# Rounding of layer 2's weights moved to chunks 1 and 8 to 10, with clamp and sign on GpSimd, and seven block products in chunk 7

## The chip, the core and the metric

The kernel runs on one core of a Trainium2 chip. The metric is device time in microseconds (us) of one execution; lower is better. TensorE does the matrix products, ScalarE, VectorE and GpSimd prepare their operands, and SyncE's queue (SP) issues nearly all transfers.

## What is computed

The reference has three stages on `x` of shape 2 x 3008 x 256 in float32:

```python
X = np.fft.rfft(x, axis=1)                      # spectral layer
Yr = Xr @ w_r - Xi @ w_i + b_r
Yi = Xr @ w_i + Xi @ w_r + b_i
Y  = sign(Y) * max(|Y| - 0.01, 0)               # on Yr and Yi
y  = np.fft.irfft(Y, n=3008, axis=1)            # 6016 tokens of 256
h = y @ w_in;  g = h / (1 + exp(-h));     y2 = g @ w_out     # layer 1, 256 -> 2048 -> 256
h = y2 @ w_in2; g = max(0.01 * h, h);     out = g @ w_out2   # layer 2, same sizes
```

## The kernel before, in words

**Arithmetic.** Every product of float32 matrices is made of three TensorE products of parts: each operand is split into a high part `hi` (rounded to the type TensorE multiplies) and the rest `lo`, and `lo*hi + hi*lo + hi*hi` is accumulated in PSUM. The high part is made by ScalarE (a cast), the low part by VectorE or GpSimd (a subtraction). The weights are first rounded to fewer bits, which takes some integer work; the change is about when and where this is done for layer 2.

**Stages.** After the forward DFT, the spectral layer and the start of the inverse DFT, the two layers run over 12 chunks of up to 512 tokens (chunk 11 has 384), each over 8 pairs of 128-wide slices of the 2048 hidden columns. The loop at L1033 counts these pairs through both layers, i = 0 to 191; chunk c of layer 1 is pairs 8c to 8c + 7. It is a software pipeline written out by hand: in the turn of pair i (`pr`) its first product is formed, pair i - 1 (`one`) is activated and split, and the second product of pair i - 2 (`two`) is accumulated. The order of calls is the order on every engine's queue.

**First product.** In an ordinary pair `first` (L723) does 2 x 6 matmuls of 512 columns. In a "quick" pair `seven` (L683) does seven block products instead of eight, in Strassen's manner: 7 x 3 matmuls of 256 columns, with sums of the weights (`sums_in`) and differences of the input (`sum_x2`, L521) prepared ahead, and with `keep` (three ScalarE copies) and `join` (two VectorE additions) to put the blocks together. Which chunks are quick is set by `FIRST_QUICK` and `LAST_QUICK` (L33, L34): 3 to 6 in layer 1, 2 to 10 in layer 2. Quick turns are written out in `quick_turn` (L974) and end with `continue`.

**Second product.** From chunk 2 of layer 1 on all chunks but the last of a layer use seven block products here (21 matmuls of 256 columns, L801). Its operands are T1 (`t1`, L769: VectorE in layer 1's chunks after the last quick one, else GpSimd), T2 and T3 (L776), T4 (L782), high parts by ScalarE (L794) and low parts (L757) by VectorE, for the group "a" by GpSimd. Chunks 0 and 1 are "plain": ScalarE casts (L762), VectorE subtracts, 12 matmuls of 512 columns. In chunk 1 GpSimd also forms sums of layer 1's weights (`sums_w1`, L588 and L601) and ScalarE and VectorE split them (L594, L595) and prepare `sums_in` (`sum_first`, L630).

**Inverse DFT.** In layer 1, `invert_next` (L571) ends the inverse for the chunk after the next in the first turns of a chunk: up to 8 small matmuls (L481), a VectorE copy (L494) and a store in a turn.

**Rounding of layer 2's weights.** They are cut into 32 pieces. A piece is loaded (`load`, L140, 256 KB, SP), ScalarE makes `c` and `m` from its two halves (L147, L149), VectorE clamps `m` (L152), shifts and masks it (L154) and puts in the sign bit of the raw data (L159), GpSimd adds `c` and `m` (L165), and SP stores the result to DRAM (L167, 128 KB). `single` (L213) does one piece in each turn from pair 55 to pair 88 (`R0`, `ROUND`, L960), the add at the start of the next turn, the rest at its end through `background` (L964). The rounded weights are loaded from DRAM by `load_m` (L947) at the pairs in `LOAD` (L958), and layer 2's sums are made from them at pairs that `PLAN` (L930) lists, counted from pair 88 on.

The memory of the weight sums (`hold0`, `hold1` of the two homes) is free once layer 1's last quick chunk has read them; `load_m` uses it for the rounded weights.

## Time and profile before

| | |
|---|---|
| median of 3 runs | 1119.71 us (1119.35 to 1120.61) |
| the profiled execution, its own time | 1119.13 us |
| its span, first to last instruction | 1117.4 us |
| TensorE busy | 1112.1 us, 100% of the span |
| VectorE busy | 950.0 us, 85% |
| ScalarE busy | 878.8 us, 79% |
| GpSimd busy | 655.0 us, 59% |

In the profile PE is TensorE's matmuls, PEld its weight loads, DVE is VectorE, ACT ScalarE, POOL GpSimd, SP SyncE. Times are in us, durations of one instruction in ns. L801 is line 801 of the kernel; where a helper issues all instructions of a kind they share its line. A releaser behind `<-` is what ended an engine's idle time. In the rows of busy times by stretch the last three columns are the granted clock of TensorE, the busy share of the DMA engines and GB/s. A matmul's end in the profile is modelled, so a TensorE that is busy for all of a stretch may still have small gaps in it.

### The profile page before, as it was taken

The page shows a single profiled execution, that of the slowest core. Times are in us where ns is not written, and L with a number is a line of the kernel's source. Part 1 is how long each engine was busy: PE and PEld are TensorE (multiplying, and loading weights), DVE is VectorE, ACT ScalarE, POOL GpSimd, SP SyncE. Part 2 cuts the span into 40 slices and gives each one's busy share as a digit, 9 for nine tenths or more (in the row PEclk, how much of TensorE's full clock was granted, in tenths as well). Part 3 has the DMA queues.
Part 4 walks back from the last instruction along what each step waited for, and adds up shares of the span by engine and source line. Part 5 has one row for each costly group of instructions (what it writes and reads, how often), then busy time and mean ns, then how long its engine had stood idle before and what let it go on. Part 6 is the DMA issues. An engine that isn't in the chain of part 4 may idle for free.

```text
span 1117.4 us, 23034 instructions
## 1 busy us (share of the span) xinstructions
PE 1112.1 (100%) x8220; PEld 1057.2 (95%) x8220; DVE 950.0 (85%) x1654; ACT 878.8 (79%) x1928; POOL 655.0 (59%) x684
## 2 busy tenths in 40 slices
PE   9999999999999999999999999999999999999998
PEld 9899888889999999999999998999999999999998
DVE  4898966578888899889999888989999999999973
ACT  4788877566788888677777777789888988988874
POOL 0567845645577565334444435756876786688652
PEclk9999999999999999999999999999999999999999
DMA  9445544123112102423344310100100101010000
GB/s 233 147 143 171 168 148 130 58 75 98 41 45 84 57 19 79 130 93 115 116 123 146 119 34 1 39 30 30 37 22 21 39 20 39 21 39 21 34 15 20
DMA packets 52547, 83.70 MB, mean 75 GB/s; under 512 B 5712, under 2 KB 27824, under 8 KB 52432
## 3 DMA queue, kind: packets, MB, share of 16 engines
q1 hardware_dynamic: 52144, 82.04, 23.9%
q8 instruction: 65, 1.06, 0.4%
q14 instruction: 50, 0.41, 0.1%
q10 hardware_dynamic: 288, 0.18, 0.1%
HBM read 52.71 MB, written 29.49 MB: 74 GB/s over the span
## 4 chain that ended last, share of the span: by engine, by line
PE 99%; DVE 0%; issue 0%; ACT 0%; POOL 0%; POOLq 0%; DVEq 0%
PE acc L801 41%; PE ph L730 20%; PE px L699 13%; PE py L699 10%; PE pz L353 6%; PE py L382 3%; PE pa L305 3%; PE px L481 2%; PE pb L405 1%; PE warm L293 0%; DVE winlo L625 0%; POOL yl L397 0%; DVE zl L366 0%; ACT ph L721 0%; DVE x L490 0%
## 5 line engine op out<-in xcount | busy, mean ns | idle before, releaser
L757 POOL TENSOR_TENSOR x<-u,x 128x512 fp32r<-128x512 f32 (+1 forms) x176 | 228.0, 1296 | 174.6 <-ACT x L794 166.7
L801 PE MATMUL acc<-x,whi 128*128 128x256 f32 (+1 forms) x1696 | 315.9, 280 | 0.0
L801 PEld LDWEIGHTS acc<-x,whi 128*128 128x128 f32 x1696 | 259.9, 189 | 0.0
L801 PE MATMUL acc<-x,wlo 128*128 128x256 f32 (+1 forms) x848 | 239.3, 282 | 0.0
L757 DVE TENSOR_TENSOR x<-v,x 128x768 fp32r<-128x768 f32 (+1 forms) x176 | 213.0, 1210 | 25.5 <-ACT x L794 24.7
L794 ACT CAST x<-v 128x768 fp32r<-128x768 f32 (+1 forms) x176 | 143.0, 813 | 48.0 <-DVE v L782 47.0
L730 PE MATMUL ph<-x,winhi 128*128 128x512 f32 (+1 forms) x704 | 179.9, 376 | 0.0
L801 PEld LDWEIGHTS acc<-x,wlo 128*128 128x128 f32 x848 | 160.4, 189 | 1.3
L730 PEld LDWEIGHTS ph<-x,winhi 128*128 128x128 f32 x704 | 130.7, 188 | 21.3
L769 POOL TENSOR_TENSOR u<-u 128x256 f32<-128x256 f32 x128 | 105.2, 822 | 59.4 <-ACT u L721 36.9
L801 PE MATMUL acc<-h,whi 128*128 128x256 f32 (+1 forms) x672 | 125.0, 279 | 0.0
L794 ACT CAST x<-u 128x512 fp32r<-128x512 f32 (+1 forms) x176 | 110.3, 627 | 3.2 <-PE acc L801 1.7
L776 DVE TENSOR_TENSOR v<-px,u 128x512 f32<-128x512 f32 x104 | 71.7, 689 | 40.8 <-ACT h L794 26.2
L730 PE MATMUL ph<-x,winlo 128*128 128x512 f32 (+1 forms) x352 | 105.4, 379 | 0.1
L801 PEld LDWEIGHTS acc<-h,whi 128*128 128x128 f32 x672 | 102.4, 189 | 2.1
L703 ACT COPY u<-px 128x256 f32<-128x256 f32 x208 | 80.0, 385 | 24.7 <-PE px L699 23.7
L165 POOL TENSOR_TENSOR wc<-wc,wm 128x256 uint32<-128x256 uint32 x64 | 49.3, 771 | 81.9 <-ACT x L794 40.2
L801 PE MATMUL acc<-h,wlo 128*128 128x256 f32 (+1 forms) x336 | 93.6, 279 | 0.0
L699 PE MATMUL px<-x,shi 128*128 128x256 f32 x416 | 81.3, 278 | 0.0
L699 PE MATMUL px<-x,winhi 128*128 128x256 f32 x416 | 81.3, 277 | 0.0
L699 PE MATMUL py<-x,shi 128*128 128x256 f32 x416 | 81.3, 277 | 0.0
L709 DVE TENSOR_TENSOR u<-py,u 128x512 f32<-128x512 f32 x104 | 71.7, 689 | 0.3 <-issue 0.3
(155 smaller groups left out, 2918.2 us busy)
## 6 DMA issues: line engine op xcount, KB each, us to landing
x2i<-scr SPq DMA_DIRECT2D x38, 256.0 KB
wraw<-in_moe_w_in_dram SPq DMA_DIRECT2D x32, 256.0 KB
wraw<-in_moe_w_out_dram SPq DMA_DIRECT2D x32, 256.0 KB
scr<-bo SPq DMA_DIRECT2D x48, 128.0 KB
scr<-x2o SPq DMA_DIRECT2D x22, 256.0 KB
out_dram<-x2o SPq DMA_DIRECT2D x22, 256.0 KB
dmr<-in_dm_dram SPq DMA_DIRECT2D x34, 160.0 KB
bt<-scr SPq DMA_DIRECT2D x14, 384.0 KB
```

The lines of the kernel that those rows point to most:

```text
L165: add.tensor_tensor(out=c, in0=c, in1=m, op=ALU.add)
L305: nc.tensor.matmul(pa[h][:, s * 128:(s + 1) * 128], lhsT=xt[c][:, s, h * 128:(h + 1) * 128], rhs=da_sb, start=True, stop=True, skip_group_ ...
L353: nc.tensor.matmul(turned(pz), lhsT=u[:, h, :], rhs=turned(v[:, h].rearrange("p g e -> p (g e)")), start=(n == 0), stop=(n == len(terms) - 1))
L699: nc.tensor.matmul(turned(out), lhsT=x, rhs=turned(y), start=(k in (1, 5) and i == 0), stop=(i == 2), skip_group_check=True)
L703: nc.scalar.copy(self.u[:, a:a + 256], src)
L709: nc.vector.tensor_tensor(out=u, in0=cols(self.py), in1=u, op=ALU.add)
L730: nc.tensor.matmul(turned(ph), lhsT=u[:, h, f % HALF * 128:][:, :128], rhs=turned(v[:, h, :]), start=(i == 0), stop=(i == len(terms) - 1))
L757: eng.tensor_tensor(out=lo, in0=src, in1=hi.bitcast(F32), op=ALU.subtract)
L769: (nc.vector if self.layer == 1 and self.c > LAST_QUICK[1] else nc.gpsimd).tensor_tensor(out=blk(1), in0=blk(0), in1=blk(2), op=ALU.subtract)
L776: nc.vector.tensor_tensor(out=cols(v), in0=b22, in1=cols(u), op=ALU.subtract)
L794: nc.scalar.copy(hi, src)
L801: nc.tensor.matmul(turned(dst), lhsT=u, rhs=turned(v), start=(begin and self.p == 0 and i == 0), stop=(end and self.p == NF // 2 - 1 and i ...
```

## The change

Layer 1's chunk 7 becomes quick (`LAST_QUICK`). The rounding of layer 2's weights gets a class of its own. Its 32 pieces are the same and come in the same order, but a piece now goes through its steps in different half turns: load; two activations on ScalarE; clamp and sign on GpSimd; one VectorE instruction that shifts `m` and puts the sign in; the add on GpSimd and the store. The sign is now made as a number: -2^31 where `m` is negative, written as an integer into the raw buffer. `round_turn` is called twice in a turn, at its start and after the first products; 5 pieces go through in pairs 8 to 15 (two sets of buffers in memory that is used otherwise from pair 16 on), 27 in pairs 64 to 90 (four sets, in the memory of the weight sums of the second home), five pieces in four pairs. The loads of `load_m(0)` come at pairs 76, 78, 80 and 82.

```diff
@@ -31,7 +32,7 @@
 NF = DFF // 128
 KT = 14
 FIRST_QUICK = {1: 3, 2: 2}
-LAST_QUICK = {1: 6, 2: 10}
+LAST_QUICK = {1: 7, 2: 10}
 
 
 def turned(a):
...
-        def single(early=False):
-            if early:
-                if scaled:
-                    around(nc.gpsimd)
-                return
-            if loaded:
-                list(begin())
-                list(scale())
-            elif not made:
-                load()
-                made.append(1)
-            load()
...
+    class Rounding:
+
+        def __init__(self, pieces):
+            self.pieces, self.loaded, self.begun, self.bound, self.scaled = pieces, [], [], [], []
+            self.n = 0
+
+        def house(self, raws, ms, cs):
+            self.raws, self.ms, self.cs = raws, ms, cs
+
+        def load(self):
+            if self.pieces:
+                src, dst = self.pieces.pop(0)
+                raw = self.raws[self.n % len(self.raws)]
+                nc.sync.dma_start(out=raw, in_=src)
+                self.loaded.append((raw, self.ms[self.n % len(self.ms)], self.cs[self.n % len(self.cs)], dst))
+                self.n += 1
+
+        def turn(self, new, more):
+            done = self.scaled
+            self.scaled = []
+            if self.bound:
+                raw, m, c, dst = self.bound.pop(0)
+                nc.vector.scalar_tensor_tensor(out=m, in0=m, scalar=3, in1=raw[:, :256], op0=ALU.logical_shift_left, op1=ALU.bitwise_or)
+                self.scaled.append((raw, m, c, dst))
+            for _ in range(more):
+                self.load()
+            for raw, m, c, dst in done:
+                nc.gpsimd.tensor_tensor(out=c, in0=c, in1=m, op=ALU.add)
+                nc.sync.dma_start(out=dst()[0], in_=c.bitcast(F32))
+            if self.begun:
+                raw, m, c, dst = self.begun.pop(0)
+                nc.gpsimd.tensor_scalar(out=m.bitcast(F32), in0=m.bitcast(F32), scalar1=MAG, scalar2=-MAG, op0=ALU.min, op1=ALU.max)
+                nc.gpsimd.tensor_scalar(out=raw[:, :256].bitcast(I32), in0=m.bitcast(F32), scalar1=0.0, scalar2=-2.0 ** 31, op0=ALU.is_lt, op1=ALU.mult)
+                self.bound.append((raw, m, c, dst))
+            if new and self.loaded:
+                raw, m, c, dst = self.loaded.pop(0)
+                two = raw.rearrange("p (e w) -> p e w", w=2)
+                nc.scalar.activation(out=c, in_=two[:, :, 0], func=ACTF.Copy, scale=2.0 ** -29)
+                nc.scalar.activation(out=m.bitcast(F32), in_=two[:, :, 1].bitcast(F32), func=ACTF.Copy, scale=2.0 ** -112)
+                self.begun.append((raw, m, c, dst))
 
     raws, late = [stage], {}
-    load_w, step_w, fifth_w, until_w = weight_pieces(
-        w_in1, w_out1, lambda k: [w_in[k][p] for p in parts] + [scr_w[:, :, k * DFF // 2:][:, :, :DFF // 2]], lambda k: [w_out[k][p] for p in parts], 2, NF)
+    load_w, step_w, fifth_w, until_w = weight_pieces(list_pieces(
+        w_in1, w_out1, lambda k: [w_in[k][p] for p in parts] + [scr_w[:, :, k * DFF // 2:][:, :, :DFF // 2]], lambda k: [w_out[k][p] for p in parts]), NF)
+    dst_m = lambda q, n: lambda k: [scr_m[q][:, k].rearrange("p (d c) -> p d c", d=2) if n else scr_m[q][:, k]]
+    rounding = Rounding(list_pieces(w_in2, w_out2, dst_m(0, 1), dst_m(1, 0)))
 
 
     fs, right = ExitStack(), ExitStack()
@@ -942,7 +969,7 @@
         if todo and (make := todo.pop(0)):
             make()
 
-    closing = []
+    closing, early = [], ExitStack()
 
     def load_m(k):
         m = [homes[k].tile([128, DFF], F32, tag=f"hold{n}", name=f"m_{q}") for n, q in enumerate(("in", "out"))]
@@ -955,21 +982,27 @@
             nc.sync.dma_start(out=m_in[k][:, :, j * 512:][:, :, :512], in_=src[0][:, :, j * 512:][:, :, :512])
             yield
 
-    LOAD = [(load_m(0), [77, 79, 81, 83]), (load_m(1), [90, 91, 92, 93])]
+    LOAD = [(load_m(0), [76, 78, 80, 82]), (load_m(1), [90, 91, 92, 93])]
     FIRST = [(sum_first(k), w) for k, w in enumerate(([10, 11, 12, 13, 13], [13, 14, 14, 15, 15], [16, 17, 17, 18, 18], [18, 19, 20, 21, 21]))]
-    R0 = 8 * LAST_QUICK[1] + 7
-    ROUND = range(R0, R0 + 34)
-    rounds = []
+    EARLY, LATE = 8, 8 * LAST_QUICK[1] + 8
+
+    def houses(tiles, n):
+        flat = [t[:, a:a + w].bitcast(U32) for t, w, k in tiles for a in range(0, w * k, w)]
+        rounding.house(flat[:n], flat[n::2], flat[n + 1::2])
+
+    def round_turn(i, half):
+        k = 2 * i + half
+        if EARLY * 2 <= k < EARLY * 2 + 16:
+            k -= EARLY * 2
+            rounding.turn(k in (2, 4, 7, 9, 12), 2 if k == 0 else k in (5, 7, 10))
+        elif LATE * 2 <= k < LATE * 2 + 54:
+            k -= LATE * 2
+            rounding.turn(k > 2 and (k % 2 == 1 or k % 8 == 0), 2 if k == 0 else k > 2 and (k % 2 == 1 or k % 8 == 0))
 
     def background(i):
-        if i == R0:
-            dst = lambda q, n: lambda k: [scr_m[q][:, k].rearrange("p (d c) -> p d c", d=2) if n else scr_m[q][:, k]]
-            rounds.append(weight_pieces(w_in2, w_out2, dst(0, 1), dst(1, 0), 1)[1])
         for steps, when in FIRST + LOAD:
             for _ in range(when.count(i)):
                 next(steps)
-        if i in ROUND:
-            rounds[0]()
 
     def quick_turn(pr, one, two, i):
         last = pr.p == NF // 2 - 1
@@ -1031,8 +1064,12 @@
             make_next()
 
     for i in range(len(pairs) + 2):
-        if rounds and i in ROUND:
-            rounds[0](True)
+        if i == 16:
+            early.close()
+            late["m4"] = pool("late4", 1, **near).tile([128, 2 * 1024 + 12], F32R, name="h1")
+        if i == LATE:
+            houses([(homes[1].tile([128, DFF], F32, tag="hold0", name="round"), 512, 4), (homes[1].tile([128, DFF], F32, tag="hold1", name="round"), 256, 8)], 4)
+        round_turn(i, 0)
         pr = pairs[i] if i < len(pairs) else None
         one, two = blocks(i - 1), blocks(i - 2)
 
@@ -1056,7 +1093,8 @@
                 both = pool("big2", 1, **near)
                 for q in parts:
                     late[q] = both.tile([128, NF // 2, 7, 128], F32R, name=f"w{q}")
-                late["m4"] = pool("late4", 1, **near).tile([128, 2 * 1024 + 12], F32R, name="h1")
+                t = pool("early4", 1, early, **near).tile([128, 2048], F32, name="round")
+                houses([(t, 512, 2), (t[:, 1024:], 256, 4)], 2)
 
         if pr and pr.quick:
             quick_turn(pr, one, two, i)
@@ -1089,6 +1127,7 @@
                 make_next()
             pr.activate(1)
             between(2 * i + 1)
+        round_turn(i, 1)
         if two:
             two.products("1")
             two.products("a")
```

## Rows read from the trace of the kernel before

**Rows 1.** The page: span, granted clock in 40 slices, shares of the chain
```profile
span 1117.4 us, 23034 instructions
...
PEclk9999999999999999999999999999999999999999
...
PE 99%; DVE 0%; issue 0%; ACT 0%; POOL 0%; POOLq 0%; DVEq 0%
```

**Rows 2.** Waits of TensorE: total us, times, longest
```profile
PE warm L293 <- DVE idle L290: 1.2, 1, 1.2
PE pb L405 <- POOL yl L397: 0.2, 1, 0.2
```

**Rows 3.** Busy times by chunk: length, then PE, PEld, DVE, ACT, POOL (instructions)
```profile
195.78:242.55 46.77, 46.77 (x225) 39.51 (x224) 29.03 (x59) 28.30 (x68) 27.80 (x43) 1.00 0.20 63
406.80:446.86 40.06, 40.06 (x354) 39.96 (x353) 36.38 (x57) 33.25 (x70) 21.21 (x21) 1.00 0.19 61
446.86:491.18 44.32, 44.32 (x298) 40.75 (x297) 40.35 (x73) 32.06 (x63) 17.68 (x18) 1.00 0.38 117
491.18:533.72 42.54, 42.54 (x283) 38.97 (x282) 39.09 (x74) 30.54 (x61) 17.90 (x18) 1.00 0.34 109
...
690.32:731.07 40.75, 40.75 (x266) 37.17 (x265) 38.74 (x61) 31.66 (x59) 27.41 (x25) 1.00 0.08 27
769.54:807.81 38.27, 38.27 (x339) 38.17 (x337) 35.29 (x56) 34.04 (x75) 28.20 (x27) 1.00 0.08 28
```

**Rows 4.** TensorE's groups by shape: inverse matmuls in chunk 7, then chunk 6
```profile
L481 PE MATMUL px<-ea_sb,bt 96*128 96x94 f32 x32 | 4.1, 271 | 0.0
...
L481 PE MATMUL px<-ea_sb,bt 96*128 96x94 f32 x16 | 2.1, 271 | 0.0
```

**Rows 5.** Groups by shape, chunks 8 to 10 (491.18 to 616.10 us)
```profile
L757 POOL TENSOR_TENSOR x<-u,x 128x512 fp32r<-128x512 f32 x24 | 30.9, 1289 | 0.0
...
L757 DVE TENSOR_TENSOR x<-v,x 128x768 fp32r<-128x768 f32 x25 | 23.9, 955 | 4.2 <-ACT x L794 3.7
L769 DVE TENSOR_TENSOR u<-u 128x256 f32<-128x256 f32 x24 | 22.9, 953 | 0.0
...
L794 ACT CAST x<-v 128x768 fp32r<-128x768 f32 x24 | 20.0, 833 | 16.5 <-DVE v L782 16.4
L165 POOL TENSOR_TENSOR wc<-wc,wm 128x256 uint32<-128x256 uint32 x24 | 17.7, 736 | 59.6 <-ACT x L794 32.2 <-ACT u L719 17.0 <-issue 8.2
...
L147 ACT ACTIVATE wc<-wraw 128x256 uint32<-128x256 uint32 x24 | 10.9, 453 | 0.0
...
L159 DVE SCALAR_TENSOR_TENSOR wm<-wraw,wm 128x256 uint32<-128x256 uint32 x24 | 10.2, 426 | 0.8
L154 DVE TENSOR_SCALAR wm<-wm 128x256 uint32<-128x256 uint32 x24 | 10.0, 415 | 0.8
L782 DVE TENSOR_TENSOR v<-v,ph 128x256 f32<-128x256 f32 x24 | 9.8, 409 | 0.0
...
L152 DVE TENSOR_SCALAR wm<-wm 128x256 f32<-128x256 f32 x24 | 8.3, 345 | 0.0
...
L510 DVE TENSOR_TENSOR x<-x2i,x 128x512 fp32r<-128x512 f32 x4 | 2.7, 678 | 0.0
```

**Rows 6.** GpSimd's groups by shape, whole execution
```profile
L267 POOL CAST dmh<-dmr 128x320 fp32r<-128x320 f32 x17 | 8.2, 482 | 0.9 <-PE pb L405 0.9
```

**Rows 7.** Timeline in chunk 9: start, us, engine, line, instruction
```profile
551.84 0.96 DVE L757 TENSOR_TENSOR x<-v,x 128x768 fp32r<-128x768 f32 x1
...
552.71 0.29 DVE L152 TENSOR_SCALAR wm<-wm 128x256 f32<-128x256 f32 x1
...
553.96 0.28 PE L801 MATMUL acc<-x,wlo 128*128 128x256 f32 x1
```

**Rows 8.** Timeline in chunk 1, pairs 12 and 13
```profile
223.47 1.28 DVE L757 TENSOR_TENSOR x<-ph,x 128x512 fp32r<-128x512 f32 x2
...
228.99 0.47 PE L801 MATMUL acc<-x,woutlo 128*128 128x512 f32 x1
```

More of the change, by code (lines that the diff above doesn't have):

```diff
@@ L12 @@
 U32 = mybir.dt.uint32
+I32 = mybir.dt.int32
 ACTF = mybir.ActivationFunctionType
@@ L116, in spectral_mlp_kernel, with list_pieces @@
     HALF = NF // 2
-    def weight_pieces(win, wout, in_dst, out_dst, n_dst, first=0):
+    def list_pieces(win, wout, in_dst, out_dst):
         win, wout = win.bitcast(U32), wout.bitcast(U32)
@@ L133, in weight_pieces @@
             pieces += new[2:] + new[:2] if q == 4 else new
+        return pieces
+    def weight_pieces(pieces, first):
         loaded, opened, begun, scaled, rounded, made = [], [], [], [], [], []
@@ L144, in begin @@
             raw, dst = loaded.pop(0)
-            m = (raws[0] if raws[1:] else late["m2"]).tile([128, 256], U32, tag="wm", name="wm", bufs=2 if raws[1:] else 1)
+            m = raws[0].tile([128, 256], U32, tag="wm", name="wm", bufs=2)
             c = stage.tile([128, 256], F32, tag="wc", name="wc", bufs=4).bitcast(U32)
@@ L165, in around @@
             add.tensor_tensor(out=c, in0=c, in1=m, op=ALU.add)
-            if n_dst == 1:
-                nc.sync.dma_start(out=dst()[0], in_=c.bitcast(F32))
             rounded.append((c.bitcast(F32), dst))
@@ L171, in split @@
             c, dst = rounded.pop(0)
-            if n_dst == 2:
-                hi, lo, *kept = dst()
-                if kept:
-                    nc.sync.dma_start(out=kept[0], in_=c)
-                nc.scalar.copy(hi, c)
-                nc.gpsimd.tensor_tensor(out=lo, in0=c, in1=hi.bitcast(F32), op=ALU.subtract)
+            hi, lo, *kept = dst()
+            if kept:
+                nc.sync.dma_start(out=kept[0], in_=c)
+            nc.scalar.copy(hi, c)
+            nc.gpsimd.tensor_tensor(out=lo, in0=c, in1=hi.bitcast(F32), op=ALU.subtract)
             made.append(1)
@@ L228, in until @@
                 step()
-        return load, (single if n_dst == 1 else step), fifth, until
+        return load, step, fifth, until
+    class Rounding:
[34 more added lines that the diff above has]
+                self.begun.append((raw, m, c, dst))
```

## Prediction

> **What bounds the kernel now.** I read the page first. Its chain of work that ended last is TensorE for 99% of the span, and the granted clock is full in every slice [rows 1]; busy TensorE alone proves little, so the list of waits comes next. It shows two waits of TensorE on another engine in the whole execution, 1.4 us together [rows 2]. Third, the busy times by chunk [rows 3]: every stretch is as long as TensorE is busy in it, while VectorE has 40.35 of 44.32 us in chunk 7 and GpSimd 17.68. So from the first layer on the time is the number of matmul columns, as long as nobody delivers late. Work taken from another engine gives nothing by itself; columns taken from TensorE give their full time.
>
> **The part that can gain: chunk 7 with seven block products.** Now a pair forms its first product with 12 matmuls of 512 columns, the same columns as 24 of 256; the quick order has 7 x 3 = 21 of 256. The second product keeps its 21. What this is worth is read from chunks that differ in nothing else. In layer 2, where no inverse DFT runs, chunk 1 (ordinary) takes 40.75 us and chunk 3 (quick) 38.27 [rows 3]: 2.48 us, or 0.31 per pair. The same by a second path: chunk 7 contains 32 inverse matmuls, chunk 6 has 16 [rows 4], and so has chunk 8 by the code; chunk 7 is 44.32 - 42.54 = 1.78 us longer than chunk 8. Chunk 6, quick, takes 40.06 with the 16, so a quick chunk 7 should take 40.06 + 1.78 = 41.84, which is 2.48 below its 44.32 [rows 3].
>
> What this adds on other engines is what chunk 6 carries today. Per pair ScalarE gets three copies, VectorE two joins, and the difference T1 goes from VectorE to GpSimd; chunk 6 must now prepare a quick successor (four differences on GpSimd, two more splits there). I cost all this at nothing: chunk 6 as it stands needs 36.38 us of VectorE and 33.25 of ScalarE in 40.06 and TensorE is busy for all of it [rows 3]. A cover lost here would show inside chunks 6 and 7.
>
> **The rounding, piece by piece.** Each of 32 pieces issues a load of 256 KB on SP, two activations, three VectorE instructions, an add on GpSimd and a store of 128 KB on SP. All of these stay but two: VectorE's clamp and mask (0.345 + 0.415 us [rows 5]) are replaced by two instructions on GpSimd. Today one piece goes with each pair from 55 on. Afterwards 5 go with pairs 8 to 15 and 27 with pairs 64 to 88, five in four pairs.
>
> TensorE side of the removal: nothing, since VectorE did not hold it up. For the new GpSimd instructions the trace has no row of this kind. Call the two together y. The nearest is the one-input cast on GpSimd, 128x320 in 0.482 us [rows 6]; by its width 256 columns are about 0.39, so I take 0.40 each and y = 0.80. The lower end is 0.77. The far upper end is a two-input operation of that size, 0.736 each [rows 5], y = 1.47. I stay with the cast because clamp and sign read one tensor each.
>
> Do chunks 8 to 10 hold that? The two engines get in each other's way: T1 on VectorE, both operands in SBUF, takes 0.953 us, while T4 of the same width, with one operand in PSUM, takes 0.409 [rows 5]; T1 is issued while GpSimd runs its 1.289 us split. So I add up what may exclude each other in these 24 pairs, 124.9 us long. VectorE: 24 x 0.955 (the 768-wide split), 24 x 0.409 (T1 alone), 6 input splits at 0.678, 27 finishing instructions at 0.426: 48.3. GpSimd: 24 x 1.289, three closings of a chunk at the same 1.289 and 0.736, 27 adds at 0.736: 56.9 [rows 5]. That is 105.2 + 27y, at y = 0.80 126.8, 1.9 over. But durations overlap: the 768-wide split starts at 551.84, lasts 0.96, and the next instruction starts at 552.71 [rows 7], 0.09 earlier than it ends. Taking 0.09 from 81 VectorE instructions leaves 97.9 + 27y = 119.5, which fits with 5.4 to spare. The cover behind that is the lead of the split: it ends at 552.80 and TensorE reads it at 553.96 [rows 7], 1.16 us. I take the second sum, so no wait; by the first, 0.7 us would appear (1.9 - 1.16).
>
> The Trainium skill, "SBUF — State Buffer", section "Who interferes with whom", states a rule that speaks against this move: a VectorE instruction with two SBUF inputs and a GpSimd instruction that reads SBUF exclude each other, and the first one holds the shared port for its whole duration. By that rule the first sum is the right one; by the row with the overlap it is the second.
>
> The new wait. VectorE's finishing instruction now waits for GpSimd's two; queued behind it are T2, T3 and the low halves that TensorE reads. It is issued half a pair after them, 2.5 us, and GpSimd has the add, the two and at most one 1.289 us split in that time: 0.736 + 0.80 + 1.289 = 2.8. A wait of 0.3 us is inside the 1.16. The new buffers: the loads of pair 64 wait for TensorE's last read of the weight sums in pair 63, and the weights loaded from pair 90 on take the same memory after the last store of pair 88; both lie pairs ahead of use.
>
> Other queues. ScalarE: two activations of about 0.453 us now stand ahead of the 768-wide cast instead of behind it; that cast waits 16.5 us in 24 pairs for T4, 0.69 each [rows 5], so at most 0.2 us of the 0.9 is late, inside the 1.16. They wait for raw data nowhere today (idle 0.0 before L147 [rows 5]); a load is still issued at least one pair ahead. SP: a store waits for GpSimd's add, and behind it are queued the next raw load, the transfers of x two pairs ahead of use, and the inverse stores; a late add of a microsecond reaches none of them. The four loads of the finished weights come one pair earlier (pairs 76 to 82 for 77 to 83); the pieces they read are stored by pairs 70 and 75. Cost nothing.
>
> Chunk 1: 5 pieces add 5 x (0.736 + 0.80) = 7.7 us to GpSimd's 27.80 and 4.5 to ScalarE's 28.30 in 46.77 us [rows 3]. In pairs 11 and 12 the activations stand ahead of the casts that TensorE's next products need, 0.9 us; the low half of pair 12 is ready at 224.75 (223.47 + 1.28) and read at 228.99 [rows 8], so 3.3 us remain. Cost nothing; without that cover, at most 2 x 0.9 = 1.8 us.
>
> **Sum.** On the profiled execution: 1119.13 - 2.48 = 1116.65 us. It lies 0.58 below the median of the runs, 1119.71, so against the median I say 1117.2. That is 0.22%, and about 0.2% (2.24 us) is what a measurement of this kernel can tell from no change: the forecast sits 0.24 us beyond that line.
>
> **Rivals.**
> 1. Forecast: columns saved, nothing late, 1117.2. Chance 0.60.
> 2. The gain is partly eaten by small waits: the first sum, without the overlap, at y between 0.80 and 0.86 (0.7 to 2.3 us), or chunk 1's 1.8. For it: VectorE is already the fullest engine beside TensorE there and its lead is only 1.16 us. Against: VectorE loses 0.76 us per piece. Time 1117.9 to 1119.5. Chance 0.24. By the Trainium skill's rule above, to the letter, it is this case with 0.7 us, 1117.9.
> 3. Slower: GpSimd's clamp and sign run at the price of two-input work. At y = 1.47 the sums are 137.6 to 144.9 against 126.1 (124.9 + 1.16), so 11.5 to 18.8 us of waits for the splits in chunks 8 to 10; in the middle 15, giving 1132. It starts to cost at y = 1.04 and turns the sign by 0.2% at y = 1.22 (4.7 us of waits, by the lower sum). For it: no row shows such an instruction here, and one of the two changes the type as well. Against: the cast does that too, at 0.482. Chance 0.12.
> 4. The quick chunk 7 saves nothing, because with four long inverse steps its engines fall behind: 1119.7. Against: chunk 6 has spare time on all of them. Chance 0.04.
>
> **How the numbers follow.** Of case 1 four fifths lies beyond the 0.2% line, given a spread of some 0.3 us between medians (the three runs lie 1.26 apart): 0.48, and with a tenth of case 2, where the wait stays under 0.24 us, faster 0.50. Same: the rest of cases 1 and 2, and case 4: 0.38. Slower: 0.12. The range 1116.5 to 1119.6 takes in cases 1 and 2 and leaves out case 3 and the far side of case 4.
>
> **What would show it.** Right: chunk 7 at about 41.8 us with 168 matmuls of L699's kind; chunks 8 to 10 as long as before (42.5, 41.6, 40.7); GpSimd's two new groups near 0.40 us each; chunk 1 at 46.8; TensorE still without waits on others. Case 2 shows chunks 8 to 10 or chunk 1 longer by tenths of a microsecond, TensorE idle ahead of the second product. Case 3 shows the new groups at 0.6 us or more and chunks 8 to 10 longer by several. Case 4 shows chunk 7 near 44. A dip of the granted clock anywhere would void the whole sum.

## The result, and the profile after

The changed kernel takes 1127.67 us in the median (1127.2 to 1128.08), the kernel before 1119.61 on the same chip (1119.32 to 1120.61): a ratio of 1.0071, 95% interval [1.0058, 1.0084], so 8.06 us slower. The forecast was 1117.2, faster. The profiled execution has a span of 1125.7 us against 1117.4, with the granted clock full in all 40 slices as before [rows 1].

First the busy times by stretch, to be held against [rows 3]: chunk 1 of layer 1, then chunks 7, 8, 9 and 10. Columns: length, then PE, PEld, DVE, ACT, POOL with their instructions, granted clock, DMA share, GB/s.

```profile
196.57:243.30 46.73, 46.73 (x226) 39.51 (x225) 30.95 (x64) 31.66 (x78) 35.89 (x54) 1.00 0.30 91
447.52:489.39 41.87, 41.87 (x371) 41.77 (x370) 37.27 (x59) 33.22 (x70) 21.26 (x21) 1.00 0.19 60
489.39:532.59 43.20, 42.80 (x283) 39.03 (x282) 35.64 (x55) 30.97 (x61) 28.88 (x30) 1.00 0.33 104
532.59:578.71 46.12, 42.88 (x274) 38.39 (x273) 40.59 (x60) 32.35 (x65) 39.18 (x41) 1.00 0.43 136
578.71:624.37 45.66, 42.07 (x266) 37.42 (x265) 39.86 (x58) 31.45 (x63) 39.10 (x41) 1.00 0.38 119
```

Chunk 7 is 41.87 us long where 41.84 was forecast, and chunk 1 is unchanged. Chunks 8 to 10 were 124.9 us and are now 43.20 + 46.12 + 45.66 = 134.98: 10.1 us more, while TensorE is no longer busy throughout. Split by the first matmul of each pair, most pairs of chunks 9 and 10 take 5.09 us before and after; the extra lies in pairs 2, 3 and 6, which take 6.4 to 7.3 us. These come right after pairs 1 and 5, in which two pieces fall, and they are where VectorE and GpSimd also close the chunk before (pairs 2 and 3) or VectorE splits the next input (pairs 5 and 6).

Second the waits of TensorE, of which there were two before [rows 2]. Columns: line, what it waited for, total us, times, longest.

```profile
PE acc L828 <- DVE x L784: 3.1, 5, 1.3
PE acc L828 <- DVE x2o L933: 1.6, 1, 1.6
PE acc L828 <- POOL x L784: 1.4, 2, 0.7
PE warm L320 <- DVE idle L317: 1.2, 1, 1.2
PE acc L828 <- ACT ph L746: 1.0, 1, 1.0
```

TensorE's second product (L828) now waits mostly for VectorE: for its 768-wide split (the low half that it makes at L784; GpSimd's low half at the same line is 512 wide), and for the closing of the chunk. The four rows at L828 make 7.1 of the 10.1 us; 2.8 more stand as busy time of TensorE, 127.75 us in these chunks against 124.92, since the ends of its matmuls are modelled. So which work on VectorE is late? Groups by shape in chunks 8 to 10 (489.39 to 624.37), first GpSimd's, then VectorE's; some records are missing, so counts reach 23 or 26 where the code has 24 or 27.

```profile
L248 POOL TENSOR_SCALAR round<-round 128x256 int32<-128x256 f32 x27 | 31.8, 1177 | 2.2
L784 POOL TENSOR_TENSOR x<-u,x 128x512 fp32r<-128x512 f32 x23 | 29.8, 1294 | 3.5 <-ACT x L821 3.5
L243 POOL TENSOR_TENSOR round<-round 128x256 uint32<-128x256 uint32 x26 | 29.5, 1133 | 6.7 <-DVE round L238 6.4 <-DMA round<-in_moe_w_out_dram 0.4
L247 POOL TENSOR_SCALAR round<-round 128x256 f32<-128x256 f32 x27 | 11.5, 424 | 2.3
...
L238 DVE SCALAR_TENSOR_TENSOR round<-round 128x256 uint32<-128x256 uint32 x26 | 32.0, 1229 | 14.5 <-POOL round L248 14.5
L784 DVE TENSOR_TENSOR x<-v,x 128x768 fp32r<-128x768 f32 x24 | 24.3, 1012 | 2.9 <-ACT x L821 2.9
```

Three things stand here. The clamp (L247) costs 0.42 us, as the cast suggested, but the sign (L248) costs 1.18. VectorE's finishing instruction (L238), 0.426 us before [rows 5], takes 1.229, and VectorE stands idle for 14.5 us ahead of it, waiting for the sign. GpSimd's add (L243) has gone from 0.736 to 1.133. The spread of sign and clamp over all 32 pieces (the view of one line; min/median/max in ns) gives the price without interference, 1.07 + 0.40 = 1.47:

```profile
L248 POOL TENSOR_SCALAR round<-round x32: 1067/1069/1657, 203.6 to 624.0; 128x256 int32<-128x256 f32 x32
...
L247 POOL TENSOR_SCALAR round<-round x32: 399/401/463, 203.1 to 623.5; 128x256 f32<-128x256 f32 x32
```

How the late sign works out is seen in the timeline at the start of chunk 9 (start, us, engine, line; in brackets the idle time before):

```profile
532.21 1.07 POOL L248 TENSOR_SCALAR round<-round 128x256 int32<-128x256 f32 x1
...
533.25 1.29 POOL L784 TENSOR_TENSOR x<-u,x 128x512 fp32r<-128x512 f32 x1
533.31 1.51 DVE L238 SCALAR_TENSOR_TENSOR round<-round 128x256 uint32<-128x256 uint32 x1 [0.40 <-POOL round L248]
534.75 0.95 DVE L784 TENSOR_TENSOR x<-v,x 128x768 fp32r<-128x768 f32 x1
534.90 1.38 POOL L243 TENSOR_TENSOR round<-round 128x256 uint32<-128x256 uint32 x1 [0.36 <-DVE round L238]
...
536.37 0.40 POOL L247 TENSOR_SCALAR round<-round 128x256 f32<-128x256 f32 x1
...
536.85 1.07 POOL L248 TENSOR_SCALAR round<-round 128x256 int32<-128x256 f32 x1
...
537.96 1.50 DVE L238 SCALAR_TENSOR_TENSOR round<-round 128x256 uint32<-128x256 uint32 x1 [0.40 <-POOL round L248]
...
539.80 1.65 POOL L248 TENSOR_SCALAR round<-round 128x256 int32<-128x256 f32 x1
...
541.43 0.73 POOL L243 TENSOR_TENSOR round<-round 128x256 uint32<-128x256 uint32 x1
541.49 0.96 DVE L238 SCALAR_TENSOR_TENSOR round<-round 128x256 uint32<-128x256 uint32 x1 [0.70 <-POOL round L248]
...
542.37 0.68 DVE L803 TENSOR_TENSOR v<-ph,u 128x512 f32<-128x512 f32 x1
```

VectorE waits 0.40 us for the sign and starts its finishing instruction 0.06 us after GpSimd began a low half of 1.29; it ends 0.28 us after that does. Its 768-wide split comes next, and GpSimd's add, which waited for the finishing instruction, is held by that split in turn. Then come the clamp and sign of the next piece. So finishing, add, clamp, sign and the next finishing form a lap between the two engines, here 537.96 - 533.31 = 4.65 us, and a pair has 5.09. At 541.49, where the pair holds two pieces, VectorE waits again, with T2 (L803) queued behind. A wait of 2.26 us follows in pair 3, behind the closing of chunk 8 on GpSimd:

```profile
553.38 1.49 DVE L238 SCALAR_TENSOR_TENSOR round<-round 128x256 uint32<-128x256 uint32 x1 [2.26 <-POOL round L248]
```

What lies between the closing and TensorE there is GpSimd's queue alone: closing, add, clamp, sign, low half, one behind the other. The first block is cut from the chain of work that ended last (start, us, engine, line), the second is TensorE's next matmul in the timeline.

```profile
549.54 1.29 POOL x2o L938
550.83 0.87 POOL round L243
...
551.79 0.40 POOL round L247
...
552.27 1.07 POOL round L248
553.34 1.25 POOL x L784
```

```profile
554.64 0.49 PE L828 MATMUL acc<-x,whi 128*128 128x256 f32 x2 [0.66 <-POOL x L784]
```

On the page this chain is now TensorE for 90% of the span and GpSimd for 5%, where it was TensorE for 99% [rows 1]. So the late sign costs in two ways: VectorE waits for it, and GpSimd comes late to its own low half behind it.

By the Trainium skill, "SBUF — State Buffer", section "Who interferes with whom", the port that the two engines share is "an exclusive lock". The trace agrees to within 0.15 us: the finishing instruction's own 0.43 us behind the 1.23 that were left of the low half would make 1.66, and it took 1.51.

### The profile page after: what moved, and what is told of

Its sections match the earlier page's. It is cut to its first block, busy times and chain, and to the rows that moved or that the text cites. A ratio compares the mean times of both kernels' runs of the same rounds, so it can differ in the third digit from the quotient of the medians.

```text
span 1125.7 us, 23245 instructions
## 1 busy us (share of the span) xinstructions
PE 1113.3 (99%) x8292; PEld 1059.7 (94%) x8292; DVE 949.9 (84%) x1598; ACT 886.5 (79%) x1958; POOL 732.3 (65%) x765
## 4 chain that ended last, share of the span: by engine, by line
PE 90%; POOL 5%; issue 2%; DVE 2%; ACT 1%; DMA 0%; POOLq 0%; DVEq 0%
PE acc L828 37%; PE ph L757 14%; PE px L726 14%; PE py L726 10%; PE pz L380 6%; PE py L409 3%; PE pa L332 3%; PE px L508 2%; POOL round L248 2%; PE pb L432 1%; POOL x L784 1%; POOL round L243 1%; POOL round L247 1%; PE warm L320 0%; POOL x2o L938 0%
## 5 line engine op out<-in xcount | busy, mean ns | idle before, releaser
L784 POOL TENSOR_TENSOR x<-u,x 128x512 fp32r<-128x512 f32 (+1 forms) x176 | 227.6, 1293 | 184.3 <-ACT x L821 177.6
L828 PE MATMUL acc<-x,whi 128*128 128x256 f32 (+1 forms) x1696 | 317.6, 281 | 4.4 <-DVE x L784 3.1
L828 PEld LDWEIGHTS acc<-x,whi 128*128 128x128 f32 x1696 | 259.9, 189 | 5.8 <-DVE x L784 4.1
L828 PE MATMUL acc<-x,wlo 128*128 128x256 f32 (+1 forms) x848 | 239.7, 283 | 2.8 <-DVE x2o L933 1.6
L784 DVE TENSOR_TENSOR x<-v,x 128x768 fp32r<-128x768 f32 (+1 forms) x176 | 217.0, 1233 | 23.4 <-ACT x L821 23.3
L828 PEld LDWEIGHTS acc<-x,wlo 128*128 128x128 f32 x848 | 160.5, 189 | 4.8 <-ACT u L746 1.8
L757 PE MATMUL ph<-x,winhi 128*128 128x512 f32 (+1 forms) x640 | 163.0, 375 | 0.0
L796 POOL TENSOR_TENSOR u<-u 128x256 f32<-128x256 f32 x136 | 111.6, 820 | 62.0 <-ACT u L748 37.0
L757 PEld LDWEIGHTS ph<-x,winhi 128*128 128x128 f32 x640 | 118.7, 188 | 19.0
L828 PE MATMUL acc<-h,whi 128*128 128x256 f32 (+1 forms) x672 | 125.0, 280 | 0.0
L803 DVE TENSOR_TENSOR v<-px,u 128x512 f32<-128x512 f32 x112 | 77.3, 690 | 45.7 <-ACT h L821 32.0
L730 ACT COPY u<-px 128x256 f32<-128x256 f32 x224 | 86.0, 384 | 29.7 <-PE px L726 28.3
L828 PEld LDWEIGHTS acc<-h,whi 128*128 128x128 f32 x672 | 102.5, 189 | 1.7
L757 PE MATMUL ph<-x,winlo 128*128 128x512 f32 (+1 forms) x320 | 95.4, 378 | 0.1
L828 PE MATMUL acc<-h,wlo 128*128 128x256 f32 (+1 forms) x336 | 93.7, 279 | 0.0
L726 PE MATMUL px<-x,winhi 128*128 128x256 f32 x448 | 87.6, 278 | 0.0
L726 PE MATMUL px<-x,shi 128*128 128x256 f32 x448 | 87.6, 278 | 0.0
L726 PE MATMUL py<-x,shi 128*128 128x256 f32 x448 | 87.6, 278 | 0.0
L784 DVE TENSOR_TENSOR h<-px,h 128x512 fp32r<-128x512 f32 x112 | 76.3, 681 | 0.0
```

The lines of the kernel that those rows point to most:

```text
L726: nc.tensor.matmul(turned(out), lhsT=x, rhs=turned(y), start=(k in (1, 5) and i == 0), stop=(i == 2), skip_group_check=True)
L730: nc.scalar.copy(self.u[:, a:a + 256], src)
L757: nc.tensor.matmul(turned(ph), lhsT=u[:, h, f % HALF * 128:][:, :128], rhs=turned(v[:, h, :]), start=(i == 0), stop=(i == len(terms) - 1))
L784: eng.tensor_tensor(out=lo, in0=src, in1=hi.bitcast(F32), op=ALU.subtract)
L796: (nc.vector if self.layer == 1 and self.c > LAST_QUICK[1] else nc.gpsimd).tensor_tensor(out=blk(1), in0=blk(0), in1=blk(2), op=ALU.subtract)
L803: nc.vector.tensor_tensor(out=cols(v), in0=b22, in1=cols(u), op=ALU.subtract)
```

## The experiments

The order is: which part costs, why the sign is dear, whether the amount of work or its order decides, and where else the work could stand. Chunk lengths are read from the trace as above.

**The rounding's move alone.** Chunk 7 stays ordinary, pieces go with the same pairs.

```diff
-LAST_QUICK = {1: 7, 2: 10}
+LAST_QUICK = {1: 6, 2: 10}
...
-    EARLY, LATE = 8, 8 * LAST_QUICK[1] + 8
+    EARLY, LATE = 8, 64
```

> Chunk 7 stays ordinary, the rounding runs as in the changed kernel (pairs 8 to 15 and 64 to 90, clamp and sign on GpSimd). If the whole loss lies in the moved rounding (my theory: GpSimd's sign at 1.07 us or more, against 0.40 estimated, makes GpSimd and VectorE run out of time in chunks 8 to 10): chunks 8 to 10 take about 10 us more than before, chunk 7 takes 44.3 again, the time is 1119.6 + 10 = 1130 us. If the loss needs the quick chunk 7 in front (its engines hand a backlog to chunk 8): about 1120.

Measured: 1129.87 us, ratio 1.0091 [1.0077, 1.0105]; chunk 7 44.32, chunks 8 to 10 43.24, 46.19, 45.67. The two parts add up: the quick chunk 7 is worth 1129.87 - 1127.67 = 2.2 us (2.45 by the chunk's length), and the whole loss belongs to the moved rounding.

**Without the sign.**

```diff
-                nc.vector.scalar_tensor_tensor(out=m, in0=m, scalar=3, in1=raw[:, :256], op0=ALU.logical_shift_left, op1=ALU.bitwise_or)
+                nc.vector.scalar_tensor_tensor(out=m, in0=m, scalar=3, in1=raw[:, :256], op0=ALU.logical_shift_left, op1=ALU.bitwise_and)
...
-                nc.gpsimd.tensor_scalar(out=raw[:, :256].bitcast(I32), in0=m.bitcast(F32), scalar1=0.0, scalar2=-2.0 ** 31, op0=ALU.is_lt, op1=ALU.mult)
```

> GpSimd's sign instruction is left out (the sign is not put in; VectorE's finishing instruction stays, with another logical operation). The two new GpSimd instructions then cost 0.42 instead of 1.5 to 1.6 us a piece. If their price decides: 97.9 + 27 x 0.42 = 109 us of 126, no waits, chunks 8 to 10 as before, 1117.1 us. If it is the new hand-over from GpSimd to VectorE, whatever it costs: at least half of the 10 us stays, 1122 or more.

Measured: 1117.57 us, ratio 0.9981 [0.9972, 0.9990]; chunks 8 to 10 42.53, 41.64, 40.74, as before the change.

**The same sign on VectorE**, ahead of the finishing instruction.

```diff
+                nc.vector.tensor_scalar(out=raw[:, :256].bitcast(I32), in0=m.bitcast(F32), scalar1=0.0, scalar2=-2.0 ** 31, op0=ALU.is_lt, op1=ALU.mult)
                 nc.vector.scalar_tensor_tensor(out=m, in0=m, scalar=3, in1=raw[:, :256], op0=ALU.logical_shift_left, op1=ALU.bitwise_or)
...
-                nc.gpsimd.tensor_scalar(out=raw[:, :256].bitcast(I32), in0=m.bitcast(F32), scalar1=0.0, scalar2=-2.0 ** 31, op0=ALU.is_lt, op1=ALU.mult)
```

> The sign is made by VectorE with the same instruction, right ahead of its finishing instruction; the clamp stays on GpSimd. If GpSimd's price decides: no waits, 1117.1 us (0.22% below before). If VectorE is the engine that runs out, some 0.3 us more per piece on it keeps waits of 2 us or more: 1119 to 1124.

Measured: 1117.80 us, ratio 0.9985 [0.9976, 0.9994], chunks as before the change. On VectorE the instruction costs less than half in the mean of chunks 8 to 10. Undisturbed it is cheaper still: the second line, of all 32 pieces, has 0.28 us in the median (min/median/max in ns), against GpSimd's 1.07.

```profile
L238 DVE TENSOR_SCALAR round<-round 128x256 int32<-128x256 f32 x27 | 13.8, 512 | 2.3 <-POOL round L248 2.3
```

```profile
L238 DVE TENSOR_SCALAR round<-round x32: 279/283/1373, 208.5 to 612.8; 128x256 int32<-128x256 f32 x32
```

So the sign on GpSimd is necessary for the loss; the clamp there is not enough for it.

**The sign without a change of type**: its output written as float32 (and the finishing instruction with `bitwise_and`).

```diff
-                nc.vector.scalar_tensor_tensor(out=m, in0=m, scalar=3, in1=raw[:, :256], op0=ALU.logical_shift_left, op1=ALU.bitwise_or)
+                nc.vector.scalar_tensor_tensor(out=m, in0=m, scalar=3, in1=raw[:, :256], op0=ALU.logical_shift_left, op1=ALU.bitwise_and)
...
-                nc.gpsimd.tensor_scalar(out=raw[:, :256].bitcast(I32), in0=m.bitcast(F32), scalar1=0.0, scalar2=-2.0 ** 31, op0=ALU.is_lt, op1=ALU.mult)
+                nc.gpsimd.tensor_scalar(out=raw[:, :256].bitcast(F32), in0=m.bitcast(F32), scalar1=0.0, scalar2=-2.0 ** 31, op0=ALU.is_lt, op1=ALU.mult)
```

> The sign instruction writes float32 instead of int32, nothing else in it changes; VectorE combines it with another logical operation (the sign is not put in rightly). If the conversion to an integer is what makes it slow: it takes about 0.42 us as the clamp does, and the time is that of the run without it, about 1117.6. If the comparison is: 1.07 us and 1127.7.

Measured: 1127.24 us, ratio 1.0068 [1.0054, 1.0081]. The group is as dear as with int32, so the type isn't the reason:

```profile
L248 POOL TENSOR_SCALAR round<-round 128x256 f32<-128x256 f32 x27 | 31.8, 1178 | 2.2
```

**The same work, half a pair earlier.** GpSimd's clamp and sign are issued right behind ScalarE's two activations, so that by the order of calls a whole half pair lies between them and VectorE's finishing instruction. With this they also come ahead of the add of another piece, no longer behind it.

```diff
+            ripe, self.begun = self.begun, []
...
-            if self.begun:
-                raw, m, c, dst = self.begun.pop(0)
-                nc.gpsimd.tensor_scalar(out=m.bitcast(F32), in0=m.bitcast(F32), scalar1=MAG, scalar2=-MAG, op0=ALU.min, op1=ALU.max)
-                nc.gpsimd.tensor_scalar(out=raw[:, :256].bitcast(I32), in0=m.bitcast(F32), scalar1=0.0, scalar2=-2.0 ** 31, op0=ALU.is_lt, op1=ALU.mult)
-                self.bound.append((raw, m, c, dst))
...
+                nc.gpsimd.tensor_scalar(out=m.bitcast(F32), in0=m.bitcast(F32), scalar1=MAG, scalar2=-MAG, op0=ALU.min, op1=ALU.max)
+                nc.gpsimd.tensor_scalar(out=raw[:, :256].bitcast(I32), in0=m.bitcast(F32), scalar1=0.0, scalar2=-2.0 ** 31, op0=ALU.is_lt, op1=ALU.mult)
                 self.begun.append((raw, m, c, dst))
+            self.bound += ripe
```

> The same instructions and buffers, but GpSimd's clamp and sign are issued in the half turn of ScalarE's two activations, half a turn earlier, and VectorE's finishing instruction where it was. If the two engines together run out of time (they exclude each other): the work is the same, most of the 10 us stays, above 1124. If VectorE only waits in its queue for a sign that comes half a turn too late: the waits go, 1117 to 1119.

Measured: 1118.10 us, ratio 0.9986 [0.9976, 0.9996]; chunks 42.54, 41.64, 41.78: 1.0 us of the 10.1 is left. VectorE's finishing instruction no longer waits, though it is still held. Chunk 10 (columns as above) shows where the rest is: VectorE is busy for its whole length.

```profile
L239 DVE SCALAR_TENSOR_TENSOR round<-round 128x256 uint32<-128x256 uint32 x26 | 29.7, 1142 | 0.0
```

```profile
572.94:614.72 41.78, 41.54 (x267) 37.44 (x265) 41.78 (x58) 31.45 (x64) 40.05 (x41) 1.00 0.41 130
```

This kernel does all that the changed one does, in the same buffers. A sum of durations gives both the same time; they are 9.6 us apart. What decides is the order of GpSimd's queue, and with it when the sign is ready; the last run below shows at which places.

**Without the clamp**: the sign stays where it is and is done one clamp earlier.

```diff
-                nc.gpsimd.tensor_scalar(out=m.bitcast(F32), in0=m.bitcast(F32), scalar1=MAG, scalar2=-MAG, op0=ALU.min, op1=ALU.max)
```

> GpSimd's clamp is left out, its sign stays (the inputs don't need the clamp for finite numbers). The sign is then done 0.49 us earlier. Theory of the late hand-over (VectorE reaches its finishing instruction, in most pairs 0.40 us before the sign is done, and queues there): VectorE's 14.5 us of waits for the sign shrink to some 4, the time is 1118 to 1120. By the sum of excluding instructions with whole durations (105.2 + 27 x 1.1 = 134.9 against 126.1) 8 to 9 us stay: 1125.

Measured: 1117.58 us, ratio 0.9980 [0.9971, 0.9989]; chunks 42.54, 41.64, 40.74. 27 clamps of 0.42 us are 11.5 us of GpSimd, and taking them out gives back all 10.1 us of TensorE. VectorE's wait for the sign shrinks from 14.5 to 4.3 us; the finishing instruction is still held, at 1.068 us, and that alone costs nothing.

```profile
L247 POOL TENSOR_SCALAR round<-round 128x256 int32<-128x256 f32 x27 | 32.9, 1219 | 0.0
...
L238 DVE SCALAR_TENSOR_TENSOR round<-round 128x256 uint32<-128x256 uint32 x27 | 28.8, 1068 | 4.3 <-POOL round L247 4.3
```

**VectorE's finishing half a pair later**, with the add, store and next load behind it.

```diff
-            self.raws, self.ms, self.cs = raws, ms, cs
+            self.raws, self.ms, self.cs, self.ripe, self.slow = raws, ms, cs, [], len(ms) == 4
...
-            if self.bound:
-                raw, m, c, dst = self.bound.pop(0)
+            ready = self.ripe if self.slow else self.bound
+            if ready:
+                raw, m, c, dst = ready.pop(0)
...
+            if self.slow:
+                self.ripe += self.bound
+                self.bound = []
...
-            rounding.turn(k > 2 and (k % 2 == 1 or k % 8 == 0), 2 if k == 0 else k > 2 and (k % 2 == 1 or k % 8 == 0))
+            rounding.turn(k > 2 and (k % 2 == 1 or k % 8 == 0), 2 if k == 0 else k > 3 and (k % 2 == 0 or k % 8 == 1))
```

> GpSimd's clamp and sign where the changed kernel has them, but in chunks 8 to 10 VectorE's finishing instruction, and with it the add, the store and the next load, half a turn later. Theory of the late hand-over: VectorE no longer waits for the sign, 1117.5 to 1119. If GpSimd's own order is what hurts (clamp and sign directly ahead of its low half, the low half late for TensorE) or the total of the two engines: above 1124.

Measured: 1123.58 us, ratio 1.0035 [1.0021, 1.0048]; chunks 8 to 11 42.53, 43.43, 44.50, 34.87, where chunk 11 took 33.86 before. So 6.6 us are left by chunk lengths and about a third of the loss is gone; neither expectation held, and the run does not settle the question, since a new wait came in. The next raw data are loaded half a pair later too, and ScalarE's activation, with TensorE's operands behind it, now stands idle for them and for a store:

```profile
L257 ACT ACTIVATE round<-round 128x256 uint32<-128x256 uint32 x27 | 12.2, 451 | 13.2 <-DMA round<-in_moe_w_out_dram 5.5 <-DMA scr_m<-round 3.3 <-DMA round<-in_moe_w_in_dram 2.7
```

**Clamp and sign both on VectorE**, ahead of the finishing instruction.

```diff
+                nc.vector.tensor_scalar(out=m.bitcast(F32), in0=m.bitcast(F32), scalar1=MAG, scalar2=-MAG, op0=ALU.min, op1=ALU.max)
+                nc.vector.tensor_scalar(out=raw[:, :256].bitcast(I32), in0=m.bitcast(F32), scalar1=0.0, scalar2=-2.0 ** 31, op0=ALU.is_lt, op1=ALU.mult)
...
-                nc.gpsimd.tensor_scalar(out=m.bitcast(F32), in0=m.bitcast(F32), scalar1=MAG, scalar2=-MAG, op0=ALU.min, op1=ALU.max)
-                nc.gpsimd.tensor_scalar(out=raw[:, :256].bitcast(I32), in0=m.bitcast(F32), scalar1=0.0, scalar2=-2.0 ** 31, op0=ALU.is_lt, op1=ALU.mult)
```

> Clamp and sign both on VectorE, with the changed kernel's places and buffers: GpSimd gets only the add, as in the kernel before. VectorE was busy 116.7 of 124.9 us in chunks 8 to 10 with 24 pieces, and 27 pieces add 3 x 1.2 us. If that fits, GpSimd was not needed at all: 1117.6. If VectorE overflows at the doubled pieces and chunk ends: waits of 1 to 4 us, 1119 to 1122.

Measured: 1118.08 us, ratio 0.9985 [0.9976, 0.9993]; chunks 42.54, 41.64, 40.90. The move in time needed no move to GpSimd.

**The clamp's time behind the sign.** GpSimd keeps the same amount of work; only the sign is one clamp earlier.

```diff
-                nc.gpsimd.tensor_scalar(out=m.bitcast(F32), in0=m.bitcast(F32), scalar1=MAG, scalar2=-MAG, op0=ALU.min, op1=ALU.max)
                 nc.gpsimd.tensor_scalar(out=raw[:, :256].bitcast(I32), in0=m.bitcast(F32), scalar1=0.0, scalar2=-2.0 ** 31, op0=ALU.is_lt, op1=ALU.mult)
+                nc.gpsimd.tensor_scalar(out=raw[:, 256:].bitcast(F32), in0=c.bitcast(F32), scalar1=MAG, scalar2=-MAG, op0=ALU.min, op1=ALU.max)
```

> GpSimd runs the sign first and an instruction with the clamp's operations and width behind it, into words that nobody reads; so the weights of layer 2 go unclamped, and GpSimd keeps all its work of the changed kernel, 32 x 1.5 us, while the sign is done one clamp, about 0.42 us, earlier. Hand-over theory (VectorE's finishing instruction waits for the sign, and then starts together with GpSimd's 1.28 us low half and is held by it): the finishing instruction has its sign before it is issued, as in the run without the clamp; chunks 8 to 10 at 42.5, 41.6 and 40.8 to 41.5 us, 1117.5 to 1118.8 us. Rival A (GpSimd's work ahead of its low half is what counts, 0.42 us too much): chunks as in the changed kernel, 43.2, 46.1, 45.7, 1127 us. Rival B (the total of what excludes each other): 1127 us too, since nothing is taken from it.

Measured: 1123.91 us, ratio 1.0034 [1.0022, 1.0047]; chunks 42.76, 44.11, 43.97. The hand-over theory and both rivals missed: 5.9 us of the 10.1 are left.

```profile
L784 POOL TENSOR_TENSOR x<-u,x 128x512 fp32r<-128x512 f32 x23 | 40.6, 1763 | 3.5 <-ACT x L821 3.5
...
L238 DVE SCALAR_TENSOR_TENSOR round<-round 128x256 uint32<-128x256 uint32 x26 | 11.7, 448 | 21.0 <-POOL round L247 20.1 <-DMA round<-in_moe_w_out_dram 1.0
```

```profile
PE acc L828 <- POOL x L784: 4.1, 4, 2.0
```

VectorE's finishing instruction is no longer held (0.448 us), since it now meets the clamp and not the low half. In exchange GpSimd's low half meets VectorE's 768-wide split, takes 1.763 instead of 1.294, and TensorE waits for that one. VectorE's wait for the sign has grown all the same, from 14.5 to 20.1 us. Of two instructions that meet here, the one that starts second pays. Here it is GpSimd that is nearly full, as chunk 9 shows (42.48 of 44.11 us):

```profile
532.58:576.69 44.11, 42.21 (x274) 38.19 (x273) 33.55 (x59) 32.37 (x67) 42.48 (x41) 1.00 0.45 142
```

**The clamp on VectorE, the sign on GpSimd.**

```diff
+                nc.vector.tensor_scalar(out=m.bitcast(F32), in0=m.bitcast(F32), scalar1=MAG, scalar2=-MAG, op0=ALU.min, op1=ALU.max)
                 nc.vector.scalar_tensor_tensor(out=m, in0=m, scalar=3, in1=raw[:, :256], op0=ALU.logical_shift_left, op1=ALU.bitwise_or)
...
-                nc.gpsimd.tensor_scalar(out=m.bitcast(F32), in0=m.bitcast(F32), scalar1=MAG, scalar2=-MAG, op0=ALU.min, op1=ALU.max)
```

> The whole rounding is there: the clamp stands on VectorE just ahead of its finishing instruction, and GpSimd keeps the sign alone, which reads the unclamped word. Hand-over theory: the sign comes 0.42 us earlier and VectorE is busy with the clamp, 0.35 us, when it would have waited; chunks 8 to 10 as before the change (42.5, 41.6, 40.8), time 1117.5 to 1118.2 us. Rival (the total): VectorE and GpSimd together have 0.08 us less per piece than the changed kernel, so the loss stays, 1125 to 1127 us. Rival 2: VectorE, with the clamp, comes to its own low halves 0.35 us later and TensorE waits for those, 1119 to 1122 us.

Measured: 1119.9 us, ratio 1.0002 [0.9993, 1.0011]; chunks 42.53, 42.20, 42.36, so 2.2 us are left. The time is in the band of the second rival, and the one wait of TensorE that came in is for VectorE's split (0.5 us). VectorE's clamp, 0.345 us before [rows 5], is now the instruction that starts beside the low half:

```profile
L238 DVE TENSOR_SCALAR round<-round 128x256 f32<-128x256 f32 x26 | 25.7, 988 | 4.3 <-POOL round L248 4.3
```

**The add behind the sign** on GpSimd, which cuts the lap.

```diff
-            for raw, m, c, dst in done:
-                nc.gpsimd.tensor_tensor(out=c, in0=c, in1=m, op=ALU.add)
-                nc.sync.dma_start(out=dst()[0], in_=c.bitcast(F32))
...
                 self.bound.append((raw, m, c, dst))
+            for raw, m, c, dst in done:
+                nc.gpsimd.tensor_tensor(out=c, in0=c, in1=m, op=ALU.add)
+                nc.sync.dma_start(out=dst()[0], in_=c.bitcast(F32))
```

> Only the order on GpSimd is another: in each half pair clamp and sign come first and the add of the piece before (with its store) behind them; all instructions, buffers and operands are those of the changed kernel. Lap theory: in the changed kernel VectorE's finishing instruction, GpSimd's add of that piece, its clamp and sign of the next piece and VectorE's next finishing instruction follow one another, a lap of 533.31 to 537.96, 4.65 us, and the pair has 5.09; with the add behind the sign that lap is cut, the sign is done an add (0.74 to 1.39 us) earlier, VectorE waits for it under 4 us in all (14.5 before), and the finishing instruction is held less. What is left is GpSimd's own work ahead of its low half, the same in sum as in the run with the clamp behind the sign: 1118 to 1124 us, chunks 8 to 10 at 125 to 131 us together. Rival A (only the sum of GpSimd's and VectorE's work counts): 1127 to 1128 us, chunks 43.2, 46.1, 45.7. Rival B (the order alone counts): chunks as before the change, 1117.6 us.

Measured: 1123.81 us, ratio 1.0037 [1.0023, 1.0051]; chunks 42.61, 44.68, 44.17, together 131.46, which is 0.5 outside the band. VectorE's wait falls from 14.5 to 6.0 us (under 4 was expected), and 3.5 us come back. So the lap is one part of the loss. The other part stays: a finishing instruction that begins beside the low half (1.084 us), a wait of 0.70 for the second sign where a pair has two pieces, and a sign that is itself held, 1.379 us.

```profile
L245 POOL TENSOR_SCALAR round<-round 128x256 int32<-128x256 f32 x27 | 37.2, 1379 | 2.2
...
L238 DVE SCALAR_TENSOR_TENSOR round<-round 128x256 uint32<-128x256 uint32 x26 | 28.2, 1084 | 6.0 <-POOL round L245 6.0
```

Held against the run with clamp and sign half a pair earlier, this run tells where that other part lies. By their traces (one record of VectorE is missing) VectorE and ScalarE run the same order in both through chunks 8 to 10, and so does GpSimd in every pair with one piece: low half, clamp, sign, add. The means are alike too (sign 1.361 there and 1.379 here, finishing instruction 1.142 and 1.084). GpSimd's order differs in eight places only. At five of them the clamp and sign of an extra piece stand ahead of a low half there and behind it here; at the three closings of a chunk one clamp and sign stand ahead of the closing there and behind it here. These eight places are worth 6.5 - 1.0 = 5.5 us, and the pairs that are longer are again 2, 3 and 6. One of the five, first there and then here:

```profile
534.84 1.13 POOL L252 TENSOR_SCALAR round<-round 128x256 int32<-128x256 f32 x1
535.93 1.28 POOL L783 TENSOR_TENSOR x<-u,x 128x512 fp32r<-128x512 f32 x1
...
538.37 1.18 POOL L252 TENSOR_SCALAR round<-round 128x256 int32<-128x256 f32 x1
```

```profile
535.62 1.46 POOL L784 TENSOR_TENSOR x<-u,x 128x512 fp32r<-128x512 f32 x1
...
537.70 1.66 POOL L245 TENSOR_SCALAR round<-round 128x256 int32<-128x256 f32 x1
...
540.16 1.07 POOL L245 TENSOR_SCALAR round<-round 128x256 int32<-128x256 f32 x1
```

## Why the prediction was wrong

**What bounds the kernel; chunk 7.** Right. TensorE's columns set the time as long as nobody is late, and the quick chunk 7 takes 41.87 us, forecast 41.84. Chunk 1 with its covers at pairs 12 and 13 held too: it is 46.73 us long, 46.77 before. The queues of ScalarE and SP held but for small waits in chunks 8 to 10: TensorE waits once for ScalarE, 1.0 us, and GpSimd once for a load, 0.4.

**The price of GpSimd's two instructions: the step that failed.** "I stay with the cast because clamp and sign read one tensor each" gave y = 0.80. The clamp bore that out at 0.40; the sign alone takes 1.07, so y = 1.47, by chance the same as the upper bound from two-input work. The number of inputs does not set the price: the clamp and the sign have the same inputs, width and number of operations, and differ by 2.7 times. The float32 form of the sign excludes the change of type. That the sign writes another buffer than it reads is not it either: the clamp in the run with the clamp's time behind the sign does so too, and its shortest takes 0.401. What is left as the difference is the comparison (or the multiplication behind it; these two were not taken apart). The Trainium skill, "GPSIMD Engine Reference", section "Engine selection", calls one-input work on GpSimd roughly line-rate. Held against VectorE the clamp fits that, 0.40 us against 0.29 [rows 7]; the sign doesn't, 1.07 against 0.28.

**The exclusion sum.** At the measured y the second sum (overlap taken off) is 97.9 + 27 x 1.47 = 137.6 against 126.1, so 11.5 us of waits, where 10.1 were measured. Its break at y = 1.04 is borne out to within a microsecond: without the clamp, at y = 1.07, it gives 0.7 us and the run shows none. So rival 3, with a chance of 0.12, was the case that came; its 1132 us came from the middle between this sum and the whole durations (18.8 us), and the lower one was nearer. But the fit is in part luck. The sum knows no order, and by it the kernels with the clamp and sign half a pair earlier, with the add behind the sign and with the clamp's time behind the sign all lose 11.5 us; they lose 1.0, 6.5 and 5.9. It says when there is danger, not what it costs.

**"The new wait."** This step named the right place, with the wrong size. It gave GpSimd 0.736 + 0.80 + 1.289 = 2.8 us against 2.5, a wait of 0.3. Measured from the add's start (534.90) to the sign's end (537.92), add, clamp and sign alone take 3.02 us instead of 1.54, because the sign is dearer and the add, which starts only after the held finishing instruction, meets VectorE's split. The step treated the wait as a single delay inside the lead of 1.16, and worked it out for a pair with one piece. It is a lap, as the timeline shows: each held instruction delays the next one on the other engine. The run with the add behind the sign gives back 3.5 us by cutting it. Where a pair carries a second piece or a chunk's closing nothing is left to catch up in: the eight places in which the last run and the one half a pair earlier differ cost 5.5 us. The split of the next input in pairs 5 and 6 was not tested by itself.

**What stays open.** All full versions that hand over in time (half a pair earlier 1118.10, sign on VectorE 1117.80, both on VectorE 1118.08) gain 1.4 to 1.7 us against before on the same chips, not 2.48, though chunk 7 gives its 2.46 or 2.47 in each. Without the clamp, where chunks 8 to 10 lose nothing at all, the gain is 1.97. Half a pair earlier, 1.0 us is lost in chunk 10, as said. For the others the traces place a part ahead of both layers: the first product of layer 1 begins at 149.96 in the trace before, and at 150.52 (sign on VectorE), 150.75 (both) and 150.76 (without the clamp). The trace before is of an execution of 1119.13 us, some 0.4 below the medians, so spread between executions is in this. In layer 2 two small shifts nearly cancel without the clamp: chunk 6 takes 38.54 us against 38.27 before, and chunk 2 38.27 against 38.47. The longer chunk 6 is in the changed kernel too (38.51), and not in the run with the rounding's move alone (38.27). None of this was tested. How much each order of the two engines costs was measured and not derived.

## What to carry to other kernels

Before work goes to an idle engine, find a row of the same operation there, or put its price at the dear end: the comparison with its multiplication cost 2.7 times a clamp of the same shape on GpSimd, and undisturbed 3.8 times the same instruction on VectorE (1.07 against 0.28). Between two engines that hold each other up the order decides, above all where a turn carries more than the usual work: the same instructions, issued half a pair earlier, cost 1 us instead of 10. And ask whether the move is needed: chunks 8 to 10 had room for all of it on VectorE, and keeping it there is faster than both kernels compared here.
